# Sliding-window attention and a squared-ReLU MLP on one core: the second group's up-projection placed ahead of the first group's down-projection, which becomes seven half-size products

## The chip, the cores and the metric

One core of a Trainium2 chip runs the whole program. The metric is the device time of one execution in microseconds (us), shown as the median of three runs. Everything below on durations comes from one profiled execution of the kernel before.

## What is computed

```python
# q, k, v: [8 batches, 8 heads, 576 positions, 64] fp32
scores = (1/8) * q @ k^T
scores = where(0 <= i - j < 128, scores - slope[head] * |i - j|, -1e9)
attn   = softmax(scores) @ v
x      = attn, heads side by side: [4608 tokens, 512]
g      = maximum(x @ w_in, 0) ** 2      # w_in: [512, 2048]
out    = g @ w_out                      # w_out: [2048, 512], out fp32
```

## The kernel before

**Blocks and groups.** A batch's 576 positions are four blocks of 128 and one of 64. The kernel numbers the 40 blocks (`seq`, L351 to L364): blocks 0 to 3 are the first blocks of batches 0 to 3, and see only themselves; a later block also sees the block before it. The MLP works on nine groups of 512 tokens. Group 0 is blocks 0 to 3, group 1 is blocks 4 to 7, group 2 begins with blocks 8 and 9.

**The work on one block.** Names as in the written-out order, `m` is the block's number. `lkq` and `lv` load k, q and v from DRAM on the POOL queue and cast them to bf16 (L590, L597). For blocks 0 to 7 TensorE transposes k and q (`tp`, L653) and ScalarE or VectorE copy them out (`ev`); from block 8 on a DMA transpose on SP's queue does that (`kqT`, L638). TensorE forms the scores (`s`, L711 or L773), ScalarE the exponentials (`e`, L734), VectorE multiplies by the mask (`m`, L742), TensorE multiplies by v (`pv`, L816), VectorE takes reciprocals and divides (`r`, `n`, L832 and L845). The result is transposed into `xT`, on TensorE with a copy (`xp` at L865, then `x`) up to block 7 and by a DMA on SP (`x`, L852) after that.

**The work on one group.** Groups 0 to 2 do the up-projection as plain products (`u`, L965, grouped by `UNITS`): `u0` works on 128 tokens at a time, `u1` and `u2` on 256. Groups 3 to 8 use seven half-size products (`f`, L1059). After each come a ReLU on ScalarE (`relu`) and a square (`sq`) on either engine. The down-projection of group 0 is plain (`o`, L1137): for each of four token blocks, four parts of four matmuls 512 columns wide, then a copy (`oe`) and a store. Groups 1 to 8 use seven half-size products (`p`, L1221), each in two halves of eight matmuls 256 columns wide, with eight sums of activations on VectorE (`S1` to `S4`, L1367), copies of partial results (`s1`, `s2`, `s3`, `s5`, L443) and combining additions (`c11`, `c12`, `c22`, L1291 to L1307). These products read `wsum`, eight sums of `w_out` made once on VectorE (`ws`, L1179).

**What sets the order.** `ORDER` (L56) lists every piece of work in sequence, with its engine (none: TensorE, `a` ScalarE, `d` VectorE, `g` POOL, `s` SP) and the PSUM banks or buffers that it takes. `Plan.order` (L269) walks through that list; each engine does its own entries strictly in this order. The costs in `plan.add` (for example the 190 ns added to scores at L717) go into times that decide only how many dummy matmuls `fill` (L420) puts in front of TensorE work during the first 30 us. There are eight PSUM banks; a bank's next user waits for the last reader of the one before. k and q go through a ring of four buffers, so a load waits until the transposes of the block four loads earlier are done.

**The first 60 us of the order before.** TensorE: scores of blocks 0 to 3, `u0`, and between them the parts of `o0`, the transposes and scores of blocks 4 to 7, then `u1`, with `s8` and the first `p1` in it. POOL: `w_in` in five pieces, with `w_out0` before and `w_out1`, `w_out2` after the last of them, `w_out3` after block 5's k and q.

Of the kernel before, what the change touches and what calls it, by code (L numbers as in the profile page):

```python
# [66 lines left out]
squ0.2.2:d squ0.1.0:d u0.3.1::3 w_out3:g o0.2.0::1 tp4.0::5 tp4.1::7 squ0.1.1:d one1.7:d ev4.1.0:d squ0.0.2:d
reluu0.3.0:a:1 mask1.5:a mask0.5:a mask1.6:a mask0.6:a reluu0.0.0:a:3 ev4.0.0:a one1.3:d squ0.0.0:d u0.1.2::4
reluu0.1.2:a:0 reluu0.3.1:a:2 us3.0:d one1.0:d u0.0.3::6 reluu0.0.3:a:3 one1.8:d u0.3.2::0 s4::2,7,5,4 mask0.2:a
mask1.3:a mask0.4:a mask0.0:a mask1.0:a e4.0:a e4.3:a squ0.1.2:d squ0.0.3:d mask0.1:a mask1.7:a mask1.1:a  # L70
mask0.7:a reluu0.3.2:a:0 squ0.3.0:d squ0.3.2:d u0.2.3::3 reluu0.2.3:a:3 mask1.4:a one1.6:d squ0.2.3:d e4.1:a
u0.1.3::6 reluu0.1.3:a:1 squ0.1.3:d lkq6:g u0.0.4::2 e4.2:a o0.2.1 u0.3.3::4 o0.1.0::0 o0.1.1 o0.1.2 ws0.0:d
one1.2:d m4.3:d one1.5:d reluu0.0.4:a:0 us1.0:d m4.1:d m4.2:d tp5.0::3 tp5.1::7 lkq7:g lv5:g lv7:g lv6:g lkq8:g
lkq9:g lv8:g m4.0:d pv4.0::6 r4.0:d pv4.1::5 n4.0:d r4.1:d n4.1:d ev5.0.0:a o0.2.2 ev5.1.0:a reluu0.3.3:a:3
s5::2,3,7,6 e5.0:a e5.3:a e5.1:a e5.2:a xp4.0::4 o0.1.3 o0.2.3 tp6.0::5 tp6.1::2 lkq10:g ev6.0.0:a oe0.1.0:a:0
oe0.2.0:a:1 o0.3.0::6 tp7.0::3 tp7.1::7 st0.1.0:s lkq11:g ws0.1:d ws1.0:d x4.0:d us3.1:d us2.0:d squ0.3.3:d
m5.0:d m5.1:d ev6.1.0:d s6::4,5,2,0 e6.0:a e6.1:a e6.2:a e6.3:a ev7.1.0:a kqT8:s lv9:g kqT9:s squ0.0.4:d
ev7.0.0:d m5.3:d m5.2:d zerov10:d zerokqT10:d us0.0:d lv10:g zerov11:d o0.0.0::1 pv5.1::3 pv5.0::4 m6.0:d m6.1:d
o0.0.1 o0.0.2 kqT10:s zerokqT11:d r5.1:d r5.0:d n5.0:d n5.1:d m6.2:d squ0.3.1:d m6.3:d ws1.2:d s7::5,2,0,7
e7.0:a pv6.0::4 xp5.0::3 x5.0:a o0.0.3 pv6.1::5 e7.2:a e7.3:a e7.1:a oe0.0.0:a:2 m7.3:d m7.1:d r6.0:d m7.0:d  # L80
r6.1:d m7.2:d kqT11:s u1.0.0::3 u1.0.2::0 u1.0.3::7 pv7.0::2 pv7.1::1 r7.0:d r7.1:d n6.0:d n7.0:d n7.1:d
# [5 lines left out]
reluu1.0.6:a:1 e9.2:a m9.0:d m9.1:d m9.3:d ws0.2:d m9.2:d p1.1.0::0 u1.0.4::6 u1.0.5::5 reluu1.0.4:a:0
reluu1.1.4:a:2 s10::2,7,1,4 pv9.1::6 pv9.0::3 p1.1.1 r9.0:d r9.1:d n9.0:d e10.0:a n9.1:d squ1.0.4:d
reluu1.0.5:a:3 e10.3:a m10.3:d squ1.0.5:d us3.3:d m10.0:d s1_1:d:4 u1.1.5::2 u1.1.0::5 lkq15:g lv14:g lv11:g
lkq16:g x9:s e10.2:a e10.1:a reluu1.1.5:a:0 squ1.1.5:a s12::3,4,6,1 e12.0:a squ1.1.4:a e12.3:a st0.2.0:s kqT13:s  # L90
kqT14:s kqT16:s kqT15:s squ1.0.6:d m10.2:d u1.1.6::7 p1.2.0::2 u1.1.7::3 m12.0:d m10.1:d e12.2:a m12.2:d m12.3:d
# [5 lines left out]
lkq17:g lkq20:g x12:s x10:s x11:s u2.0.4::3 p1.5.0::5 reluu2.0.4:a:1 p1.5.1 s14::4,2,7,6 s5_1:a:5 e14.0:a
e14.1:a e14.2:a m13.2:d m13.0:d m13.1:d S4.1.0:d p1.6.0 pv13.0::3 u2.0.3::4 squ2.0.6:d squ2.0.4:d us1.1:d
m14.1:d r13.0:d m14.2:d n13.0:d m14.0:d reluu2.0.3:a:3 e14.3:a reluu2.0.1:a:1 squ2.0.0:a squ2.0.7:d p1.6.1
pv13.1::2 p1.3.0 r13.1:d n13.1:d m14.3:d s2_1:a:6 s15::7,3,4,6 pv14.0::1 pv14.1::2 r14.0:d r14.1:d us0.1:d  # L100
n14.0:d n14.1:d squ2.0.3:d lv15:g lkq18:g lkq19:g lv17:g lv18:g p1.7.0 p1.7.1 e15.0:a e15.3:a e15.2:a e15.1:a
s16::7,6,1,4 m15.0:d e16.0:a u2.1.2::2 e16.1:a e16.2:a reluu2.1.2:a:0 e16.3:a kqT17:s kqT20:s st1.2.1:s x14:s
x13:s kqT19:s u2.1.0::3 m15.1:d pv15.0::7 u2.1.3::6 reluu2.1.3:a:2 reluu2.1.0:a:3 c22_1:d us0.3:d m16.0:d
m15.2:d m15.3:d pv15.1::1 m16.1:d pv16.0::2 r16.0:d n16.0:d squ2.0.1:d r15.0:d r15.1:d p1.4.0 u2.0.2::4
u2.1.1::6 n15.0:d m16.3:d n15.1:d s17::3,2,7,1 reluu2.0.2:a:1 squ2.1.0:a m16.2:d pv16.1::4 squ2.0.2:d r16.1:d
p1.4.1 e17.0:a n16.1:d e17.3:a e17.2:a reluu2.1.1:a:1 m17.2:d squ2.1.1:d m17.3:d kqT18:s st1.2.0:s x15:s
st0.3.0:s x16:s lv19:g lkq22:g lkq21:g lkq23:g lv21:g lv20:g lkq26:g u2.1.5::3 u2.1.4::4 p1.3.1 reluu2.1.5:a:3
e17.1:a squ2.1.2:a squ2.1.5:d m17.0:d us1.3:d m17.1:d reluu2.1.4:a:1 squ2.1.3:a squ2.1.4:d c12_1:d S1.2.0:d
u2.1.7::1 u2.1.6::7 pv17.0::6 p2.1.0::3 us1.2:d S3.2.0:d r17.0:d reluu2.1.7:a:3 squ2.1.7:a reluu2.1.6:a:0
squ2.1.6:a s3_1:a:7 us0.2:d S1.2.1:d n17.0:d S2.2.1:d pv17.1::2 s18::4,5,1,7 e18.0:a e18.3:a m18.0:d ut3.0:d  # L110
p2.1.1 e18.1:a p2.2.0::0 p2.2.1 m18.1:d S2.2.0:d ut3.1:d m18.3:d ut3.2:d e18.2:a s1_2:a:0 f3.0.5::6 f3.0.1::4
p2.6.0 s5.3.0:a:1 S4.2.1:d us3.2:d r17.1:d m18.2:d s1.3.0:a:4 p2.6.1 ut3.3:d S3.2.1:d f3.0.6 f3.0.2::7
c11.3.0:d:1 p2.5.0::5 pv18.1::1 pv19.0::7 f3.0.3 s2.3.0:a:3 c11_2:d us2.2:d n17.1:d f3.0.7 pv18.0::0 s2_2:a:4
p2.7.0 p2.5.1 c12.3.0:d:2 reluc12.3.0:d c22.3.0:d:3 reluc11.3.0:a sqc11.3.0:a p2.7.1 r18.0:d r19.0:d sqc12.3.0:a
reluc22.3.0:a f3.1.1::2 s5_2:a:3 sqc22.3.0:a s1.3.1:a:1 n18.0:d S4.2.0:d r18.1:d n18.1:d n19.0:d st0.0.0:s
kqT21:s st1.3.0:s kqT22:s pv19.1::6 c22_2:d r19.1:d n19.1:d f3.0.4 kqT23:s x17:s st1.3.1:s x18:s x19:s f3.1.2::0
# [1313 lines left out]
```

## Time and profile before

| | us |
|---|---|
| median of 3 runs | 295.35 (294.89 to 295.40) |
| the profiled execution | 293.89 |
| its span, first to last instruction | 292.1 |
| TensorE busy in the span | 282.8 |
| VectorE busy | 247.1 |
| ScalarE busy | 226.9 |
| POOL busy | 106.5 |

The profiled execution lies 1.46 us below the median of the timed runs, and 1.8 us of it lie outside the span. Busy times are sums of the records of an engine. Records of matmuls overlap, since a matmul starts before the one ahead has drained: how fast a stream of them runs is read from the distance between starts, or from a merged piece of the chain (its length over its matmuls), not from the mean record.

### The profile page before, as it was taken

The page shows a single profiled execution, that of the slowest core. Times are in us where ns is not written, and L with a number is a line of the kernel's source. Part 1 is how long each engine was busy: PE and PEld are TensorE (multiplying, and loading weights), DVE is VectorE, ACT ScalarE, POOL GpSimd, SP SyncE. Part 2 cuts the span into 40 slices and gives each one's busy share as a digit, 9 for nine tenths or more (in the row PEclk, how much of TensorE's full clock was granted, in tenths as well). Part 3 has the DMA queues.
Part 4 walks back from the last instruction along what each step waited for, and adds up shares of the span by engine and source line. Part 5 has one row for each costly group of instructions (what it writes and reads, how often), then busy time and mean ns, then how long its engine had stood idle before and what let it go on. Part 6 is the DMA issues. An engine that isn't in the chain of part 4 may idle for free.

```text
span 292.1 us, 8683 instructions
## 1 busy us (share of the span) xinstructions
PE 282.8 (97%) x3443; PEld 238.5 (82%) x3443; DVE 247.1 (85%) x645; ACT 226.9 (78%) x445; POOL 106.5 (36%) x132
## 2 busy tenths in 40 slices
PE   5889999999999999999999999999999999999994
PEld 2589766788888888888888888888898888888884
DVE  4444588877798699999999999999999898999883
ACT  3658967688789695899999999899886957858710
POOL 8954377393265372912573630820000000000000
PEclk9999999999999999999999999999999999999999
DMA  9999999999999999999999999998500523010225
GB/s 124 166 199 195 190 167 179 145 130 141 180 167 143 179 207 171 131 139 173 185 173 141 142 197 154 168 168 139 116 3 5 152 80 91 1 41 20 90 81 154
DMA packets 170921, 39.64 MB, mean 136 GB/s; under 512 B 156928, under 2 KB 170368, under 8 KB 170880
## 3 DMA queue, kind: packets, MB, share of 16 engines
q0 software_dynamic: 115184, 18.10, 95.1%
q1 hardware_dynamic: 54800, 20.26, 37.6%
q10 hardware_dynamic: 896, 0.72, 1.0%
q8 instruction: 27, 0.44, 0.6%
q14 instruction: 14, 0.11, 0.1%
HBM read 36.70 MB, written 9.44 MB: 158 GB/s over the span
## 4 chain that ended last, share of the span: by engine, by line
PE 87%; DMA 8%; POOL 4%; issue 0%; ACT 0%; DVE 0%; POOLq 0%
PE o L1221 33%; PE h L1059 26%; PE h L965 13%; PE pv L816 6%; PE s L711 5%; DMA vf<-in_v_dram 3%; DMA kqT<-kq 3%; PE o L1137 2%; DMA kq<-in_q_dram 2%; POOL kq L590 2%; POOL vf L597 1%; POOL w_in_sb L535 1%; PE o L1323 1%; PE xp L865 0%; PE tp L653 0%
## 5 line engine op out<-in xcount | busy, mean ns | idle before, releaser
L734 ACT ACTIVATE P<-s 128x512 bf16<-128x512 f32 x120 | 65.6, 612 | 5.2 <-PE s L711 4.9
L1221 PEld LDWEIGHTS <-g 128*128 128x128 bf16 x624 | 60.0, 98 | 7.0
L590 POOL DMA_DIRECT2D kq<-in_k_dram x39 | 33.9, 868 | 69.4 <-DMA kqT<-kq 65.6
L932 ACT ACTIVATE rt<-h 128x512 bf16<-128x512 f32 (+1 forms) x73 | 42.3, 600 | 14.7 <-PE h L965 9.9
L1080 DVE TENSOR_TENSOR rt<-h,f 128x512 bf16<-128x512 f32 x72 | 48.7, 686 | 4.1 <-PE h L1059 1.3
L924 ACT ACTIVATE g<-rt 128x512 bf16<-128x512 bf16 x80 | 48.9, 636 | 1.4 <-DVE rt L1085 0.7
L1221 PE MATMUL o<-w_out_sb,g 128*128 128x256 bf16 x384 | 47.7, 273 | 0.0
L965 PE MATMUL h<-xT,w_in_sb 128*128 128x128 bf16 (+1 forms) x512 | 46.4, 246 | 0.0
L443 ACT ACTIVATE f<-h 128x512 f32<-128x512 f32 x59 | 34.9, 606 | 11.1 <-PE h L1059 10.9
L965 PEld LDWEIGHTS <-w_in_sb 128*128 128x128 bf16 x512 | 38.9, 98 | 3.9
L1059 PE MATMUL h<-xT,w_in_sb 128*128 128x256 bf16 x288 | 41.4, 273 | 0.1
L1059 PEld LDWEIGHTS <-w_in_sb 128*128 128x128 bf16 x384 | 35.8, 98 | 5.2 <-issue 0.3
L742 DVE TENSOR_TENSOR P<-P,masks 128x512 bf16<-128x512 bf16 x96 | 37.1, 420 | 2.2 <-ACT P L734 2.1
L597 POOL DMA_DIRECT2D vt<-in_v_dram x36 | 30.8, 876 | 16.6 <-PE pv L816 9.0
L590 POOL DMA_DIRECT2D kq<-in_q_dram x39 | 33.7, 865 | 5.7 <-DMA w_out_sb<-in_moe_w_out_dram 2.3
L926 DVE TENSOR_TENSOR g<-rt 128x512 bf16<-128x512 bf16 (+1 forms) x65 | 26.1, 415 | 6.9 <-ACT rt L932 6.6
L845 DVE TENSOR_TENSOR x<-pv,rec 128x256 bf16<-128x256 f32 (+1 forms) x80 | 31.4, 414 | 0.5
L1221 PE MATMUL o<-wsum,sums 128*128 128x256 bf16 x256 | 31.7, 273 | 0.0
L1221 PE MATMUL o<-wsum,g 128*128 128x256 bf16 x240 | 30.5, 273 | 0.0
L1059 PEld LDWEIGHTS <-us 128*128 128x128 bf16 x288 | 27.1, 98 | 3.7
L1087 ACT ACTIVATE rt<-rt 128x512 bf16<-128x512 bf16 x38 | 24.1, 637 | 5.6 <-DVE rt L1080 5.2
L816 PEld LDWEIGHTS <-P 128*128 128x128 bf16 (+1 forms) x576 | 24.0, 100 | 5.0 <-issue 2.3
(81 smaller groups left out, 398.3 us busy)
## 6 DMA issues: line engine op xcount, KB each, us to landing
out_dram<-f SPq DMA_DIRECT2D x54, 128.0 KB, 2.6
kq<-in_k_dram POOLq DMA_DIRECT2D x31, 128.0 KB, 5.9
kq<-in_q_dram POOLq DMA_DIRECT2D x31, 128.0 KB, 6.5
vt<-in_v_dram POOLq DMA_DIRECT2D x28, 128.0 KB, 7.0
w_out_sb<-in_moe_w_out_dram POOLq DMA_DIRECT2D x4, 512.0 KB, 14.5
w_in_sb<-in_moe_w_in_dram POOLq DMA_DIRECT2D x3, 512.0 KB, 10.2
out_dram<-f SPq DMA_DIRECT2D x4, 256.0 KB, 5.0
out_dram<-f SPq DMA_DIRECT2D x13, 64.0 KB, 2.1
```

Source lines behind the costliest of these rows:

```text
L443: nc.scalar.activation(o, i, AF.Copy)
L590: nc.gpsimd.dma_start(view(kq[s_kq[m].idx], i), source(src, m, split))
L597: nc.gpsimd.dma_start(tile_of(s_v[m])[0:n, :, 0:D], source(v, m))
L734: nc.scalar.activation(flat(Pt[sP.idx]), sS[i].tile.rearrange("p (j t) -> p j t", j=2)[:, :, lo:hi], AF.Exp, bias=0.0, scale=scale)
L742: nc.vector.tensor_tensor(flat(Pt[sP.idx]), flat(Pt[sP.idx]), flat(masks), op=ALU.mult)
L816: nc.tensor.matmul(sv.tile[0:n, hi * (D + 1):(hi + 1) * (D + 1)], prob, tile_of(s_v[mk])[:, h, 0:D + 1], start=mk == parts[0][1], stop=mk ...
L924: nc.scalar.activation(o, i, AF.Square, bias=0.0, scale=1.0)
L932: nc.scalar.activation(rts[srt.idx][:, 0:n], slot.tile[:, 0:n], AF.Relu, bias=0.0, scale=1.0)
L965: nc.tensor.matmul(slot.tile[:, f * w:(f + 1) * w], w_in_sb[:, cc, fc * 128:(fc + 1) * 128], xT[:, cc, lo % (XR * 128):lo % (XR * 128) + w ...
L1059: nc.tensor.matmul(slot.tile[:, j * 256:j * 256 + 256], a, b_, start=fresh and j == 0 and c == 0, stop=c == 1, skip_group_check=True)
L1080: nc.vector.tensor_tensor(rts[srt.idx], slot.tile, other(), op=ALU.add)
L1221: nc.tensor.matmul(slot.tile[:, z * 256:z * 256 + 256], stationary(c), moving(c), start=fresh and z == 0 and c == 0, stop=c == F - 1, skip ...
```

## The change

1. `G_STR` goes from 1 to 0, so that group 0's down-projection is done as the seven half-size products too. The 16 `o0` parts, four `oe0` copies and four full-width stores go; 14 `p0` halves, eight sums `S1` to `S4`, four copies, three combining additions and eight half-width stores come.
2. `ORDER` is written anew from end to end. In the first part all of `u0` and nearly all of `u1` stand ahead of `p0`; the transposes and scores of blocks 4 to 7 stand between the units of `u0`; `p1` follows `p0`.
3. On POOL the `w_out` pieces move behind the loads of blocks 4 to 7 and 9.
4. In the later groups some copies, ReLUs and squares change between ScalarE and VectorE (over the whole list 50 entries go from VectorE to ScalarE and 46 the other way). Block 0's cast of k goes to ScalarE.
5. Small edits: one 'stage' buffer for block 0's k and q becomes four entries over the same tensor `wsum` (block 0 uses the first, in the same place as before); the 190 ns in the cost of scores go; an option `SPLIT` is added and is off.

The core of the diff, with the part of the order up to the first products, as far as the prediction speaks of it:

```diff
-G_STR = 1
+G_STR = 0
...
-e1.1:a ev0.0.0:a cq0:d tp0.1::5 lv2:g pv2.0::6 r2.0:d ev0.1.0:d lv1:g lkq3:g lv0:g w_in0:g w_in1:g w_in2:g lv3:g
-w_in3:g w_out0:g lkq4:g w_in4:g w_out1:g w_out2:g lkq5:g lv4:g pv1.0::7 pv1.1::0 pv2.1::2 r1.1:d r1.0:d n1.0:d
...
+slope0.3:d cq0:d lkq1:g lv0:g lv1:g lv2:g lkq3:g w_in0:g tp2.0::1 tp0.0::2 tp0.1::3 tp2.1::4 tp1.0::5 tp1.1::6
+w_in1:g w_in2:g lv3:g w_in3:g lkq4:g lkq5:g w_in4:g lkq6:g slope1.2:a slope0.1:a slope0.0:a slope1.3:a
...
+n0.0:d b3::5,6 tp3.0::1 tp3.1::3 r2.0:d n2.0:d r0.1:d one0.1:d pv1.0::4 n0.1:d r2.1:d n2.1:d ev3.0.0:d lv4:g
+lv5:g lkq7:g lv6:g xp0.0::7 pv1.1::2 xp2.0::0 r1.1:d r1.0:d x2.0:d ev3.1.0:a s3 e3.0:a u0.2.0::3 n1.0:d n1.1:d
+x0.0:d xp1.0::1 mask1.1:a e3.1:a mask1.5:a x1.0:a u0.0.1::0 u0.0.0::4 u0.1.0::5 mask1.0:a reluu0.0.1:a:0
+reluu0.2.0:a:1 mask1.4:a reluu0.1.0:a:2 pv3.1::2 u0.0.2::7 pv3.0::6 u0.2.1::1 u0.1.1::0 dist0:d r3.0:d r3.1:d
+n3.0:d n3.1:d one1.5:d squ0.1.0:d xp3.0::3 u0.1.2::5 tp4.0::6 tp4.1::2 reluu0.2.1:a:3 squ0.2.0:d squ0.2.1:d
...
+mask0.2:a mask1.7:a reluu0.1.2:a:2 mask1.6:a ev4.0.0:d ev4.1.0:d squ0.0.1:d one1.2:d u0.2.2::1 s4::7,3,0,4
+mask0.1:a reluu0.2.2:a:0 mask0.7:a mask1.2:a e4.0:a e4.2:a mask0.6:a e4.1:a lkq9:g lv7:g w_out2:g tp5.0::6
+tp5.1::5 u0.0.3::2 u0.3.0::1 squ0.1.1:d ev5.1.0:d one1.8:d one1.7:d squ0.0.0:d one1.3:d ev5.0.0:d squ0.2.2:d
+us3.0:d one1.0:d mask0.4:a us3.1:d m4.0:d one1.1:d s5::7,5,0,6 reluu0.0.3:a:1 e4.3:a one1.4:d m4.2:d m4.3:d
+m4.1:d squ0.0.3:d e5.0:a reluu0.3.0:a:3 e5.2:a e5.1:a u0.1.3::3 u0.3.1::2 reluu0.3.1:a:0 e5.3:a tp6.0::4
+tp6.1::7 ev6.0.0:d ev6.1.0:d squ0.3.0:d u0.3.2::1 pv4.0::0 reluu0.3.2:a:1 s6::5,2,4,7 pv4.1::6 u0.2.3::1 e6.0:a
+e6.2:a e6.1:a m5.1:d m5.3:d r4.0:d m5.0:d n4.0:d r4.1:d m5.2:d n4.1:d pv5.0::5 tp7.0::0 reluu0.2.3:a:3 ev7.0.0:a
+e6.3:a pv5.1::4 m6.0:d m6.1:d r5.0:d squ0.2.3:d u0.0.4::6 xp4.0::2 tp7.1::1 reluu0.0.4:a:3 pv6.0::0 x4.0:a
+ev7.1.0:a u0.3.3::7 r5.1:d n5.0:d m6.2:d n5.1:d r6.0:d m6.3:d n6.0:d xp5.0::5 pv6.1::6 s7::4,2,0,1 x5.0:a
+lkq10:g w_out0:g w_out1:g lkq8:g squ0.3.1:d r6.1:d reluu0.3.3:a:0 n6.1:d squ0.0.4:d e7.0:a e7.3:a e7.1:a e7.2:a
+m7.0:d squ0.1.2:d squ0.3.3:d m7.1:d u1.0.3::5 u1.0.0::6 u1.0.2::7 kqT9:s m7.3:d m7.2:d us1.0:d zerokqT10:d
+kqT10:s xp6.0::4 x6.0:d u1.0.6::1 pv7.0::2 squ0.3.2:d us2.0:d r7.0:d n7.0:d pv7.1::0 u1.0.5::4 reluu1.0.3:a:3
+reluu1.0.0:a:2 squ1.0.0:a reluu1.0.6:a:0 reluu1.0.5:a:2 r7.1:d n7.1:d u1.0.4::5 xp7.0::6 u1.0.1::1 u1.0.7::2
+ws0.2:d ws0.0:d x7.0:d squ1.0.5:d w_out3:g kqT8:s lv9:g lv8:g lkq11:g lkq12:g lkq13:g lkq14:g lv12:g lv13:g
+reluu1.0.7:a:1 squ1.0.3:a squ1.0.6:a u1.1.1::0 u1.1.6::4 reluu1.1.1:a:2 reluu1.1.6:a:3 squ1.1.6:a reluu0.1.3:a:0
+S1.0.0:d u1.1.5::6 squ1.0.7:d reluu1.1.5:a:1 u1.1.3::2 u1.1.2::0 S1.0.1:d us0.0:d S3.0.1:d zerov10:d zerokqT11:d
+squ1.1.5:a u1.1.0::4 p0.1.0::3 u1.1.7::6 reluu1.1.3:a:3 us2.1:d ws0.1:d squ0.1.3:d S2.0.0:d squ1.1.3:d S3.0.0:d
...
+reluu1.0.2:a:0 squ1.0.1:d ws1.1:d reluu1.1.7:a:1 squ1.1.7:a p0.2.0::2 p0.2.1 s8::5,1,4,0 c11_0:d u1.1.4::7
+p0.5.0::6 p0.5.1 kqT11:s squ1.0.2:d S2.0.1:d S4.0.0:d e8.0:a e8.1:a e8.3:a e8.2:a m8.1:d m8.0:d s9::2,5,1,0
...
-            t = plan.add({"PE": 190.0 + len(grps) * 2 * len(pieces) * mm(128 if n == 128 else 64)}, due - 32, scores,
+            t = plan.add({"PE": len(grps) * 2 * len(pieces) * mm(128 if n == 128 else 64)}, due - 32, scores,
```

More of the change, by code (lines that the diff above doesn't have):

```diff
@@ L18 @@
 N_HW = 1
+SPLIT = False
 N_PE = 8
@@ L67 @@
[L67 to L81, printed above, removed]
@@ L87 @@
[L87 to L91, printed above, removed]
@@ L97 @@
[L97 to L116, printed above, removed]
@@ new lines @@
+S4.1.1:d r10.1:d r10.0:d n11.1:d n10.0:d n10.1:d p1.6.0 s13::1,0,2,4 e13.0:a e13.1:a e13.2:a e13.3:a kqT15:s
+st0.3.1:s x11:s x10:s st0.2.1:s x12:s u2.0.7::6 p1.5.0::5 p1.5.1 s14::1,0,2,4 reluu2.0.6:a:1 reluu2.0.7:a:3
+e14.0:a e14.2:a s5_1:a:5 p1.6.1 e14.3:a e14.1:a m13.3:d m13.0:d m13.1:d m13.2:d S4.1.0:d pv13.0::3 s2_1:d:6
+r13.0:d u2.0.0::6 u2.0.1::1 pv13.1::2 m14.2:d reluu2.0.0:a:0 squ2.0.0:a m14.1:d m14.0:d u2.0.4::4 reluu2.0.1:a:0
+lv17:g lv15:g lkq20:g lkq18:g lkq19:g n13.0:d squ2.0.7:d r13.1:d n13.1:d S3.1.1:d squ2.0.6:a p1.3.0 pv14.0::0
@@ new lines @@
+r14.0:d s15::6,3,1,2 m14.3:d n14.0:d us0.1:d p1.7.0 p1.7.1 reluu2.0.4:a:3 e15.0:a e15.3:a e15.2:a e15.1:a
+kqT17:s st0.3.0:s st0.2.0:s st0.4.2:s st0.7.3:s x13:s kqT18:s kqT20:s kqT19:s s16::4,0,6,2 u2.0.2::1 u2.1.2::3
+e16.0:a e16.2:a e16.1:a e16.3:a m15.0:d c22_1:d m15.3:d m15.2:d pv15.1::4 u2.1.3::6 pv14.1::0 m16.1:d m15.1:d
+squ2.0.4:d m16.0:d reluu2.0.2:a:1 reluu2.1.3:a:3 squ2.0.3:a reluu2.1.2:a:2 squ2.1.2:a pv15.0::2 p1.4.0 pv16.0::1
+u2.1.1::6 m16.3:d r15.0:d r14.1:d n15.0:d n14.1:d r15.1:d n15.1:d us0.3:d r16.0:d squ2.0.2:d m16.2:d n16.0:d
@@ new lines @@
+s17::2,0,3,4 p1.4.1 lkq21:g squ2.0.1:d reluu2.1.1:a:2 u2.1.4::6 pv16.1::1 e17.0:a m17.0:d us1.1:d us1.3:d
+r16.1:d n16.1:d e17.2:a x14:s x15:s st1.2.1:s x16:s st1.2.0:s st0.7.2:s squ2.1.1:d e17.3:a u2.1.0::2
+reluu2.1.4:a:1 squ2.1.4:a reluu2.1.0:a:0 e17.1:a squ2.1.3:a lv19:g lv18:g lkq23:g lkq22:g m17.1:d m17.2:d
+us3.3:d squ2.1.0:d u2.1.5::3 u2.1.6::4 reluu2.1.5:a:1 squ2.1.5:d S1.2.0:d u2.1.7::6 p1.3.1 reluu2.1.6:a:2
+reluu2.1.7:a:3 s3_1:a:7 squ2.1.7:a squ2.1.6:a lv21:g lv20:g lkq26:g s18::1,2,0,3 pv17.0::4 e18.0:a e18.2:a
@@ new lines @@
+r18.1:d pv18.0::4 r18.0:d ut3.3:d f3.1.2::5 f3.1.1::2 sqc11.3.0:a reluc12.3.0:a s2_2:a:1 p2.7.0 pv19.1::0
+sqc12.3.0:a s1.3.1:a:3 reluc22.3.0:a f3.0.4 f3.1.6 p2.7.1 S4.2.0:d c11.3.1:d:2 r19.1:d n18.0:d n18.1:d
+sqc22.3.0:a reluf3.0.4:a:0 lkq24:g lkq25:g s20::5,4,3,7 st1.3.0:s x18:s x17:s s2.3.1:a:3 reluc11.3.1:a n19.1:d
+x19:s c22_2:d sqc11.3.1:d f3.1.5::0 s5.3.1:d:4 f3.1.7 p2.3.0 e20.0:a e20.3:a e20.1:a e20.2:a m20.0:d f3.1.3
+m20.3:d c22.3.1:d:1 m20.2:d p2.4.0 m20.1:d reluc22.3.1:a sqf3.0.4:a sqc22.3.1:a c12.3.1:d:3 pv21.1::5 pv20.1::7
@@ new lines @@
+f6.0.3 S1.5.1:d ut6.2:d S2.5.1:d f6.0.7 e36.0:a e36.2:a e36.3:a e36.1:a p5.6.0 p5.6.1 s37::5,3,7,4 S4.5.0:d
+c11_5:d ut6.3:d c22.6.0:d:0 reluc22.6.0:d c12.6.0:d:1 e37.0:a e37.3:a f6.0.4 f6.2.1::0 f6.1.2::1 f6.1.1::5
+e37.1:a s1.6.1:a:0 e37.2:a reluf6.0.4:a:2 p5.5.0::4 x32:s st4.4.3:s st4.2.1:s st4.4.2:s st3.2.1:s st3.2.0:s
+x34:s st4.3.0:s st5.2.1:s x33:s x31:s x35:s st4.3.1:s st4.7.2:s p5.5.1 f6.1.6 S3.5.1:d sqc22.6.0:d c11.6.1:d:0
+m36.0:d sqf6.0.4:d m37.3:d m37.2:d S4.5.1:d m36.3:d s2_5:a:5 s2.6.1:a:0 s38::3,7,1,6 e38.0:a e38.3:a p5.7.0
@@ L214 @@
+s2_8:d:4 st7.7.3:s st7.4.3:s c12_7:d st7.3.0:s st7.3.1:s p8.7.0 p8.7.1 st7.2.1:s st8.2.1:a st8.2.0:s s5_8:a:7
+c22_8:d st8.7.3:a st8.7.2:a s3_8:d:6 p8.3.0 p8.3.1 c12_8:d st8.3.1:s st8.3.0:a p8.4.0::7 c21.0.0_8:d st8.4.0:s
+p8.4.1::2 c21.1.0_8:d st8.4.1:s p8.4.1b::6 c21.1.128_8:d st8.4.1b:a
 """
@@ L407 @@
     xt = ring("x", size["x"], [128, d_model])
-    stages = [wsum.rearrange("p s c t -> p (s c t)")[:, 0:4 * d_model].bitcast(FP32)]
-    plan = Plan({"b": 8, "f": NF, "rt": RT, **{f"g{f}.{t}": 2 for f in range(FCB) for t in range(2)}, "rec": 4, "ut": UT, "s1": 1, "s2": 1, **{f"v0.{i}": 1 for i in range(L)}, "kqT0": L, "stage": 2, **size})
+    stages = [x.rearrange("p c t -> p (c t)").bitcast(FP32) for x in (wsum[:, i] for i in range(4))]
+    plan = Plan({"b": 8, "f": NF, "rt": RT, **{f"g{f}.{t}": 2 for f in range(FCB) for t in range(2)}, "rec": 4, "ut": UT, "s1": 1, "s2": 1, **{f"stage{i}": 1 for i in range(4)}, **{f"v0.{i}": 1 for i in range(L)}, "kqT0": L, **size})
     def bank(slot, name):
@@ L566, in load_block, with fetch @@
         if split:
-            s_st = Slot("stage")
             t_l = []
+            s_st = Slot(f"stage{m % 4}")
             for i, src in enumerate((k, q)):
-                for r, (eng, e) in enumerate((("SP", nc.sync), ("SP", nc.sync) if m else ("ACT", nc.scalar))):
-                    def fetch(i=i, src=src, r=r, e=e):
-                        e.dma_start(view(stages[s_st.idx], i)[:, r], source(src, m, split)[:, :, r])
-                    t_l.append(plan.add({eng: 740.0}, key + 0.1 * i, fetch, [], [] if t_l else [s_st], dma=330.0,
-                                        lat=(1100.0 if m else 1500.0) + 600.0 * (r if m else i * (1 - r)),
+                for r in range(2):
+                    def fetch(i=i, src=src, r=r):
+                        e = nc.scalar if t_l[2 * i + r].eng == "ACT" else nc.sync
+                        e.dma_start(view(stages[m % 4], i)[:, r], source(src, m, split)[:, :, r])
+                    t_l.append(plan.add({("SP", "ACT")[r]: 720.0} if m == 0 else {"SP": 720.0, "ACT": 720.0},
+                                        key + 0.1 * i, fetch, [], [] if t_l else [s_st], dma=330.0, lat=1500.0,
                                         name=f"l{'kq'[i]}{m}.{r}", after=t_l[0] if t_l else None))
@@ L580, in cast_kq @@
                      kq[s_kq[m].idx][:, w].rearrange("s (i r d) -> s r i d", i=4, d=D),
-                     stages[s_st.idx][:, w].rearrange("s (r i d) -> s r i d", r=2, d=D))
-            engs = {"DVE": 350.0, "ACT": 480.0} if m else {"DVE": 350.0}
+                     stages[m % 4][:, w].rearrange("s (r i d) -> s r i d", r=2, d=D))
+            engs = {"DVE": 350.0, "ACT": 480.0}
             c_q = None
@@ L652, in tp @@
                 for j in range(C):
-                    nc.tensor.transpose(st.tile[:, j * 128:(j + 1) * 128],
-                                        src[:, j * 128:(j + 1) * 128], ident)
+                    nc.tensor.transpose(st.tile[:, j * 128:(j + 1) * 128], src[:, j * 128:(j + 1) * 128], ident)
             t_tp[i] = plan.add({"PE": 4 * mm(128)}, due - 60 + i, tp,
@@ L697, in job @@
         t_s = [None, None]
-        bursts = [[0, 1]]
+        bursts = [[0], [1]] if SPLIT else [[0, 1]]
         for z, grps in enumerate(bursts):
@@ L774, in scores @@
                                      tile_of(s_kqT[m])[rows, C + c, :], start=False, stop=c == C - 1)
-        t_s = plan.add({"PE": 190.0 + 4 * mm(128)}, due - 32, scores, [t_b] + t_kqT[m], name=f"s{m}")
+        t_s = plan.add({"PE": 4 * mm(128)}, due - 32, scores, [t_b] + t_kqT[m], name=f"s{m}")
         t_bias.append(t_b)
```

220 lines of the change are left out of this document (104 added, 116 removed).

## The prediction

> **What bounds the kernel now.** I read the page's busy times and slices first, then the chain that ended last (its sum, then its pieces in order of time), then TensorE's waits and timeline, then the busy times by stretch.
>
> ```profile
> PE 282.8 (97%) x3443; PEld 238.5 (82%) x3443; DVE 247.1 (85%) x645; ACT 226.9 (78%) x445; POOL 106.5 (36%) x132
> ...
> PE   5889999999999999999999999999999999999994
> ...
> PEclk9999999999999999999999999999999999999999
> ...
> PE 87%; DMA 8%; POOL 4%; issue 0%; ACT 0%; DVE 0%; POOLq 0%
> ```
>
> From the third slice (15 us) to the last TensorE is busy all the time at full clock, and 87% of the chain is TensorE. Overlapping records could hide gaps, so I look at the pieces:
>
> ```profile
> 11.50 8.59 DMA vf<-in_v_dram
> ...
> 20.53 1.79 PE h L965 x32
> ...
> 30.11 0.55 PE s L711 x16
> ...
> 34.31 0.89 PE h L965 x16
> 35.20 2.59 PE o L1137 x12
> 37.79 0.45 PE tp L653 x8
> ...
> 41.52 6.22 DMA kq<-in_q_dram
> ...
> 47.76 7.36 DMA kqT<-kq
> ...
> 275.29 11.36 PE o L1221 x104
> ```
>
> Each piece of matmuls divided by its count is the streaming rate: 56 ns at 128 columns (1.79/32), 109 at 256 (11.36/104), 216 at 512 (2.59/12). The other pieces run at these rates, so TensorE has no room. It waits in two places after its start:
>
> ```profile
> 20.13 0.40 PE L816 MATMUL pv<-vf,P 128*128 128x65 bf16 x8 [0.52 <-DMA vf<-in_v_dram]
> ...
> 55.16 0.23 PE L711 MATMUL s<-kqT,kqT 64*128 64x128 bf16 x2 [0.17 <-DMA kqT<-kq]
> ```
>
> At 20.13 block 3's v has just landed (11.50 + 8.59 = 20.09), and at 55.16 block 8's transposed k and q (47.76 + 7.36 = 55.12). Between and behind them lies one stream of work. So a change is worth what it takes from TensorE's stream after 20 us, less every wait that it adds there.
>
> **What goes and comes on TensorE.** `o0` is 64 matmuls of 512 columns: 64 x 216 = 13.8 us. `p0` is 14 x 8 = 112 of 256 columns: 112 x 109 = 12.2 us. On the path: -1.6 us. Changes between scores, `pv` and other matmuls cost about 0.1 us each (scores begin 0.1 us after the piece ahead of them ends); their number in the two orders differs by four, so I count nothing.
>
> The mean weight load is 98 ns, and one precedes every matmul. It fits below the 109 ns of a 256-column matmul, and the 104 matmuls above show it hidden. The Trainium skill ("TensorE: Matmul & The Clock Gate", section "Back-to-back issue gap") gives 81 ns per matmul for sustained streams with weight loads at 128 columns and 131 ns at 512. By a straight line between these, an estimate, `p0` would take 112 x 98 = 10.9 us and `o0` 64 x 131 = 8.4, so the change would lose 2.6 us. The rows above (56, 109, 216) disagree at every width.
>
> **What comes on the other engines.** ScalarE: four copies for four copies, nothing. VectorE: eight sums and three combining additions, records of 0.69 us, in a row 0.6 us apart: 11 x 0.6 = 6.6 us. They lie beside TensorE as long as VectorE keeps ahead of it.
>
> ```profile
> 50.00:55.00 5.00, 4.99 (x56) 4.08 (x54) 3.77 (x14) 3.61 (x7) 0.65 (x1) 1.00 1.82 153
> ...
> 60.00:65.00 5.00, 5.00 (x64) 4.42 (x62) 3.64 (x13) 4.42 (x9) 5.00 (x7) 1.00 2.11 136
> ...
> 160.00:200.00 40.00, 40.00 (x524) 34.31 (x523) 39.44 (x107) 37.52 (x73) 15.88 (x19) 1.00 1.80 162
> ```
>
> The columns are TensorE, weight loads, VectorE, ScalarE, POOL. Around 50 to 65 us VectorE is busy three quarters of the time by records that overlap a little; by its groups it idles some 22 us between 20 and 120 us, which covers 6.6. From 120 to 200 us it is nearly full and gains no work. If that cover is gone, the price is what VectorE lacks, up to 6.6 us. SP gets four more stores, behind `kqT15` and among the `x` transposes; an issue takes about 0.6 us, and blocks 10 to 16 queue behind them, far ahead of their scores. Nothing counted; one late transpose would cost under 1 us.
>
> **The start.** The new order there (k of block 0 cast on ScalarE, v ahead of block 3) ends at the same point: the same loads stand ahead of block 3's v on POOL, so it lands at 20.1 again, and TensorE has the same work done by then with the 0.52 us wait as cover. Nothing; if the start slips by more than 0.5 us, the excess is paid.
>
> **The moved loads.** Landings in the trace come 0.85 us apart for one of a block's k, q or v, half that for a 64-row block, and 2.55 us for a 512 KB weight piece, without a gap from 5 to 50 us. In the new sequence from 20.1: `w_in3` 22.6, block 4's q 24.3, block 5's 26.0, `w_in4` 28.6, block 6's q 30.3, v4 and v5 32.0, block 7's q 33.7, v6 34.5, block 9 36.2, v7 37.1, `w_out2` 39.6, block 10 40.5, `w_out0` 43.1, `w_out1` 45.6, block 8's q 47.3, `w_out3` 49.9.
>
> Against that, TensorE's list from 20.13 at rates of the chain (unit of `u0` 0.89, pair of `tp` 0.45, scores 0.55 + 0.1, half a `pv` 0.2 to 0.3, `xp` 0.22, unit of `u1` 0.87):
> - up to `tp4.1`, which needs block 4's q: four units, two `pv`, `xp`, one `tp` = 4.4, so 24.5 against 24.3;
> - to `tp5.1`: 2.0 more, 26.5 against 26.0;
> - to `tp6.1`: 4.65 more, 31.15 against 30.3;
> - to `tp7.1`: 5.2 more, 36.35 against 33.7;
> - to `p0.1.0`, which needs `w_out0` and `w_out1`: 15.85 more, 52.2 against 45.6;
> - to `p0.2.0` with `w_out3`: 2.6 more, 54.8 against 49.9;
> - to `s8`: 1.75 more, 56.6 against block 8's transposes, 47.3 + 7.36 = 54.7.
>
> Every load is there first, the first two by 0.2 and 0.5 us. ScalarE's list between 18.3 and 38 us (14 ReLUs and 16 exponentials and copies at 0.48, 13 masks at 0.2, two short ReLUs) is 17.7 us in 19.7: it runs up to 3 us behind TensorE, and by the bank numbers each bank still comes free 0.2 us or more before its next user. I take +0.2 us for these narrow places, with bounds of 0 and 1.5. The 0.17 us wait of `s8` goes; block 8 comes next late, 1.9 us away.
>
> **Sum.** -1.6 - 0.17 + 0.2 = about -1.5 us: the profiled execution's 293.89 becomes 292.4, and the median of the runs, which lies 1.46 higher, 295.35 - 1.5 = **293.9**. About 0.2%, or 0.6 us, is what a measurement can tell from no change.
>
> **Rivals.**
> - *Narrow places eat the gain.* Each of the four transposes waits on a load that must keep its pace, and ScalarE's lag holds banks. Waits of 0.9 to 2.1 us in all give 294.8 to 295.9. For it: margins of 0.2 and 0.5 us. Against: loads keep their spacing to a few hundredths, and a wait at `tp4.1` widens the margins behind it.
> - *Slower: block 8's transposes become the wait.* Its load now stands behind three `w_out` pieces, and `kqT9` and `kqT10` go ahead on SP while loads are in flight. If these two take 1.3 us each of the DMA engines (the issue record of a transpose), block 8 lands at 49.9; with the longest time to landing in the trace, 9.4 us, `s8` starts at 59.3 in place of 56.6: +2.7, and 296.6. Scores of later blocks queue behind the same transposes and could double it. It decides from a landing at 58.8 on (2.2 us late). Against: 7.36 us with eight loads in flight is the nearest row. The Trainium skill ("DMA: Bandwidth & Descriptors", section "Queues, rings and completion order") says that each DMA engine goes round its queues by packets, which fits 7.36 us beside loads.
> - *Slower: VectorE's 6.6 us are not covered.* If half meets TensorE's needs before 120 us, +3.3: 297.2. For it: it is full from 120 on. Against: 22 us of idle time ahead of that.
> - *TensorE's work does not shrink* because weight loads are not hidden between `p0` halves: 48 more loads x 98 ns = 4.7 us, so 295.35 + 4.7 - 1.5 = 298.5. The skill's rule of the sustained gap points this way; all `p` rows speak against it.
>
> **How the numbers follow.** Forecast 0.60, its own range 292.9 to 294.7; eaten gain 0.14; block 8 0.12; VectorE 0.12; no shrinking 0.02. So faster 0.60, same 0.14, slower 0.26. The range runs from 292.9 to 297.0: left out are a little of the forecast (0.03), the doubled wait (0.03), half of VectorE's case (0.06) and the last (0.02).
>
> **What will show it.** Right: L1137 gone, 112 more matmuls on L1221 at 109 ns, no TensorE wait over 0.2 us between 20 and 60 us, block 3's v at 20.1. Wrong: `tp` waiting for k or q loads, `s` at L711 waiting for `kqT`, or matmuls after 60 us waiting for VectorE; a start of the stream later than 20.6 would break the step on the start.

## The result, and the profile after

| | before | changed |
|---|---|---|
| median of 22 runs each, us | 295.14 (293.66 to 296.01) | 295.88 (294.05 to 298.15) |
| the profiled execution, us | 293.89 | 295.96 |
| its span, us | 292.1 | 294.2 |

The ratio of the times is 1.0036, with a 95% interval of 1.0018 to 1.0053: slower, by 0.7 us between the medians and 0.36% by the ratio. The prediction, 293.9, had the direction wrong; its range, 292.9 to 297.0, holds 295.88 only by what it gave to the rivals. Between the two profiled executions the gap is 2.1 us; that of before is one of its shorter ones. In the experiments a few executions ran clearly longer than the others (two of e4's six, two of e14's twelve): the medians take in all executions, the ratios and intervals leave these out.

The page of the changed kernel, from its busy times, its 40 slices and its chain:

```profile
PE 284.0 (97%) x3514; PEld 246.3 (84%) x3514; DVE 250.6 (85%) x651; ACT 228.7 (78%) x449; POOL 106.4 (36%) x132
...
PE   4899999989999999999999999999999999999995
...
PEclk9799999999999999999999999999999999999999
...
PE 83%; DMA 9%; DVE 5%; issue 1%; ACT 0%; ACTq 0%; DVEq 0%; SPq 0%
```

There are 71 more TensorE records than in the profile of before: 48 by the products (112 in place of 64) and 23 more dummy matmuls of `fill` (50 in place of 27); the 7 in the second slice of the clock and the ninth slice of PE (59 to 66 us) are new. The timeline of TensorE names every wait of 0.2 us or more that is behind the warm-up, and shows where block 3's `pv` begins:

```profile
6.35 0.40 PE L655 MATMUL tp<-ident,kq 128*128 128x128 bf16 x4 [0.62 <-DMA kq<-in_k_dram]
8.66 1.46 PE L655 MATMUL tp<-ident,kq 128*128 128x128 bf16 x12 [1.91 <-ACT kq L444]
...
21.97 0.23 PE L817 MATMUL pv<-vf,P 128*128 128x65 bf16 x2
...
59.90 0.23 PE L712 MATMUL s<-kqT,kqT 64*128 64x128 bf16 x2 [1.43 <-DMA kqT<-kq]
```

Two waits are new. At 8.66 TensorE has waited 1.91 us for block 0's k, whose second half is now the second load on ScalarE's queue (landing 6.60; in the kernel before the first, 3.76) and whose cast on ScalarE has the 1.28 us loading of its table between. Block 3's v has landed at 19.90, but TensorE gets to it at 21.97 in place of 20.13. And at 59.90 block 8's scores have waited 1.43 us for their transposes. Of the chain, in order of time, the pieces that lead there and some of `p0` behind:

```profile
37.16 13.73 DMA kq<-in_q_dram
...
50.96 8.89 DMA kqT<-kq
59.85 0.05 issue
59.90 0.62 PE s L712 x16
```

```profile
61.50 1.75 PE o L1222 x16
64.39 3.49 PE o L1222 x32
```

Block 8's q was issued at 37.16 and landed at 50.90; its transposes landed at 59.85. From there TensorE hardly waits to the end: 294.2 - 59.9 = 234.3 us, where the prediction had 290.6 - 56.6 = 234.0. So the whole miss lies ahead of `s8`, which starts 3.3 us later than forecast. The pieces of `p0` run at 109 ns (3.49 over 32), as its step said.

**Theory** for the experiments: block 8's transposes set the start of `s8`, because the DMA transposes of blocks 9 and 10, in flight on SP's queue from 36.7 and 41.0 us, slow the loads that block 8 needs. **Rivals**: the late start is what costs the time; the loads' order does; VectorE's added work does; the products save nothing.

### The profile page after: what moved, and what is told of

It reads as the page before. It is cut to its first block, busy times and chain, and to the rows that moved or that the text cites. A ratio compares the mean times of both kernels' runs of the same rounds, so it can differ in the third digit from the quotient of the medians.

```text
span 294.2 us, 8852 instructions
## 1 busy us (share of the span) xinstructions
PE 284.0 (97%) x3514; PEld 246.3 (84%) x3514; DVE 250.6 (85%) x651; ACT 228.7 (78%) x449; POOL 106.4 (36%) x132
## 3 DMA queue, kind: packets, MB, share of 16 engines
q1 hardware_dynamic: 55248, 20.13, 39.3%
## 4 chain that ended last, share of the span: by engine, by line
PE 83%; DMA 9%; DVE 5%; issue 1%; ACT 0%; ACTq 0%; DVEq 0%; SPq 0%
PE o L1222 35%; PE h L1060 23%; PE h L966 9%; PE pv L817 6%; PE s L712 5%; DMA kq<-in_q_dram 5%; DMA kqT<-kq 3%; DMA wsum<-in_k_dram 2%; DVE rt L1081 1%; PE tp L655 1%; PE tp L423 1%; PE s L765 1%; PE o L1324 1%; DVE P L743 1%; PE s L774 0%
## 5 line engine op out<-in xcount | busy, mean ns | idle before, releaser
L1222 PEld LDWEIGHTS <-g 128*128 128x128 bf16 x704 | 67.5, 98 | 8.2
L735 ACT ACTIVATE P<-s 128x512 bf16<-128x512 f32 x120 | 64.0, 616 | 5.4 <-PE s L712 5.4
L925 ACT ACTIVATE g<-rt 128x512 bf16<-128x512 bf16 x88 | 53.2, 631 | 1.3 <-DVE rt L1086 0.5
L1222 PE MATMUL o<-w_out_sb,g 128*128 128x256 bf16 x432 | 54.1, 273 | 0.0
L1222 PE MATMUL o<-wsum,sums 128*128 128x256 bf16 x288 | 36.2, 273 | 0.0
L1222 PE MATMUL o<-wsum,g 128*128 128x256 bf16 x272 | 34.8, 273 | 0.0
L1222 PEld LDWEIGHTS <-sums 128*128 128x128 bf16 x288 | 27.7, 98 | 3.3
L444 ACT ACTIVATE f<-o 128x512 f32<-128x512 f32 x30 | 17.9, 597 | 13.4 <-PE o L1222 13.4
L1088 ACT ACTIVATE rt<-rt 128x512 bf16<-128x512 bf16 x40 | 25.2, 635 | 3.0 <-DVE rt L1081 2.9
```

Source lines behind the costliest of these rows:

```text
L444: nc.scalar.activation(o, i, AF.Copy)
L735: nc.scalar.activation(flat(Pt[sP.idx]), sS[i].tile.rearrange("p (j t) -> p j t", j=2)[:, :, lo:hi], AF.Exp, bias=0.0, scale=scale)
L925: nc.scalar.activation(o, i, AF.Square, bias=0.0, scale=1.0)
L1222: nc.tensor.matmul(slot.tile[:, z * 256:z * 256 + 256], stationary(c), moving(c), start=fresh and z == 0 and c == 0, stop=c == F - 1, skip ...
```

## The experiments

Each stands beside runs of the kernel before on its own chip; the ratio is to those. There are 12 executions of each, but 6, 5 and 4 of e4, e5 and e6.

| kernel | median us | ratio, 95% interval |
|---|---|---|
| e1_start_back | 296.68 | 1.0050 (1.0028 to 1.0072) |
| e4_block8_load | 299.25 | 1.0102 (1.0054 to 1.0149) |
| e5_both | 300.94 | 1.0211 (1.0184 to 1.0239) |
| e6_both_no_dummies | 301.26 | 1.0218 (1.0188 to 1.0247) |
| e7_transposes_behind | 294.17 | 0.9989 (0.9967 to 1.0011) |
| e8_behind_and_start | 294.17 | 0.9992 (0.9965 to 1.0020) |
| e9_plain_o0 | 296.31 | 1.0046 (1.0023 to 1.0069) |
| e10_no_late_dummies | 294.64 | 1.0008 (0.9985 to 1.0032) |
| e11_changed_again | 295.97 | 1.0035 (1.0017 to 1.0053) |
| e12_block10_behind | 295.68 | 1.0044 (1.0014 to 1.0074) |
| e13_block10_and_start | 295.59 | 1.0031 (1.0004 to 1.0059) |
| e14_behind_again | 294.59 | 0.9989 (0.9959 to 1.0018) |
| e15_load8_between | 295.42 | 1.0011 (0.9983 to 1.0038) |
| e16_load8_between_start | 295.11 | 1.0011 (0.9985 to 1.0038) |

### The start taken back

```diff
-... lk0.0:s lq0.1:a one0.0:d warm0:d warm::0 lkq2:g lk0.1:a lq0.0:s ck0:a
+... lk0.0:s lk0.1:a one0.0:d warm0:d warm::0 lkq2:g lq0.0:s lq0.1:a ck0:d
```

> The changed kernel with two edits of its start taken back: block 0's k halves are both loaded ahead of its q halves, and its cast goes back to VectorE. Start theory (the stream is late at block 3's v, 21.97 instead of 20.13 us, only because TensorE waits 1.91 us for that cast and then runs at a granted clock of 0.50 from 9 to 12 us): no wait for the cast, clock 1.00 from 5 us on, block 3's `pv` begins by 20.6, and, if nothing behind it holds the gain back, 1.8 us less: 294.1. Together with the block 8 theory (block 8's scores start when its transposes land, 59.85 us, and these depend on the DMA queues and not on TensorE): the 1.4 us wait of `s8` grows to about 3.2, `s8` still starts at 59.9, and the time stays within 0.4 us of the changed kernel's. Rival (the time is lost to VectorE's added sums or behind 60 us): block 3's `pv` is earlier, the wait of `s8` does not grow, and the gain vanishes at waits for VectorE.

The timeline of TensorE in this kernel (e1), and then its busy times around 60 us (TensorE, weight loads, VectorE, ScalarE, POOL, granted clock, DMA share, GB/s):

```profile
20.06 0.28 PE L817 MATMUL pv<-vf,P 128*128 128x65 bf16 x4 [0.52 <-DMA vf<-in_v_dram]
59.24 0.23 PE L712 MATMUL s<-kqT,kqT 64*128 64x128 bf16 x2 [2.70 <-DMA kqT<-kq]
```

```profile
58.00:60.00 2.00, 0.76 (x17) 0.56 (x18) 0.88 (x2) 0.32 (x1) 0.27 (x1) 0.89 2.20 153
60.00:62.00 2.00, 2.00 (x12) 1.45 (x11) 0.99 (x3) 1.77 (x5) 2.00 (x3) 0.50 1.36 121
```

The start is whole again: block 3's `pv` at 20.06 (21.97 as changed) with the 0.52 us wait of the kernel before. The wait of `s8` grows from 1.43 to 2.70, and `s8` begins only 0.66 us earlier. So the late start is not what the time was lost to: block 8's transposes are a floor that TensorE reaches sooner or later. I had not expected that even the 0.66 us would be lost. The second fence shows it: after the longer wait the granted clock is 0.50, and from `s8` to the next block's scores it takes 4.90 us (59.24 to 64.14) in place of the changed kernel's 3.28 (59.90 to 63.18), 1.6 more. This execution is 1.1 us longer than the changed kernel's (spans of 295.3 and 294.2). Over all executions a rise is not shown: the ratios to the kernel before are 1.0050 and 1.0036, with intervals that overlap.

### Block 8's load earlier, alone and with the start, and without dummies

```diff
-lkq10:g w_out0:g w_out1:g lkq8:g
+lkq10:g lkq8:g w_out0:g w_out1:g
```

> The changed kernel with the load of block 8's q and k put ahead of the first two pieces of w_out instead of behind them. Block 8 theory: the load lands some 7 to 8 us earlier (about 43 in place of 50.9), its transposes by 53, the 1.43 us wait of `s8` goes, the span falls by 1.4 us and the time to about 294.5. Price to watch: w_out's second piece lands up to 2 us later (48.35 to 50.2), while the first `p0` that needs it begins at 53.9, so nothing. Rival (the transposes of block 8 are slow because of the loads beside them, wherever its load stands): `s8` still waits over 1 us and the time does not move.

> Both edits together: the start taken back and block 8's load ahead of w_out. If the start (1.84 us) and block 8's wait (1.43 us) are all that the prediction missed, apart from dummy matmuls (about 0.4 us), the time falls by 3.3 us to about 292.6, 2.5 below the kernel before, and the profile shows no TensorE wait over 0.2 us from 20 to 62 us. Rival (VectorE's eight sums and three combinations, 6.6 us, are not covered): TensorE waits for VectorE appear, and the time stays at 294.5 or more.

The last one (e6) has `FILL = 0.0` as well:

> As the last one, with all dummy matmuls left out (52 of them, 7 behind 20 us). The seven behind 20 us stand in the stream and cost 7 x 56 ns = 0.4 us. Those ahead of it either fill waits (then taking them out gives nothing, and the waits become idle time) or delay the stream. Theory: 0.4 us less, about 292.2. Rival: with more idle time in the first 20 us the granted clock falls to 0.50 there as it did in the changed kernel, and the time rises by 0.5 to 1.7 us.

All three missed. Timelines, first TensorE's and VectorE's with block 8's load moved (e4), then the same two with both edits (e5):

```profile
50.06 5.40 PE L966 MATMUL h<-xT,w_in_sb 128*128 128x256 bf16 x48 [1.47 <-DVE xT L442]
```

```profile
48.38 1.29 DVE L1180 TENSOR_TENSOR wsum<-w_out_sb 128x1024 bf16<-128x1024 bf16 x2 [2.35 <-DMA w_out_sb<-in_moe_w_out_dram]
```

```profile
53.46 7.28 PE L966 MATMUL h<-xT,w_in_sb 128*128 128x256 bf16 x48 [6.46 <-DVE xT L442]
```

```profile
51.78 1.29 DVE L1180 TENSOR_TENSOR wsum<-w_out_sb 128x1024 bf16<-128x1024 bf16 x2 [7.34 <-DMA w_out_sb<-in_moe_w_out_dram]
```

The wait of `s8` is gone in both, and a worse one stands in its place. I had looked for the first user of `w_out` on TensorE (`p0` at 53.9). The first on VectorE is `ws0.2`, at 46, and the copy `x7` that TensorE needs for `u1` stands behind it in VectorE's list. w_out's first piece lands at 48.36 in the one and 51.75 in the other (44.25 as changed). The times of e4 spread from 296.19 to 302.37, and its profile is of the shortest, so how long this wait mostly is isn't seen. In e5, w_out's first piece is spread over eight microseconds: the first of its 16 parts lands at 43.43, the last at 51.75, with block 9's transpose in flight beside it (36.28 to 50.32). e6 waits 6.64 us at the same place; its granted clock stays at full speed in the first 20 us, so the drop that its rival had there did not come, but what the dummies are worth can't be read from a kernel with such a wait. What follows: the order of the loads can't be mended by moving block 8's alone, since w_out's first piece has no slack either.

### The transposes of blocks 9 and 10 behind block 8's

```diff
-... u1.0.2::7 kqT9:s m7.3:d m7.2:d us1.0:d zerokqT10:d
-kqT10:s xp6.0::4 ...
+... u1.0.2::7 m7.3:d m7.2:d us1.0:d
+xp6.0::4 ...
-w_out3:g kqT8:s lv9:g
+w_out3:g kqT8:s kqT9:s zerokqT10:d kqT10:s lv9:g
```

> The changed kernel with SP's DMA transposes of blocks 9 and 10 put behind that of block 8; its start and its loads stay as changed. Transpose theory (a DMA transpose in flight takes turns with the loads packet by packet: beside block 9's, the two w_out pieces landed 4 us apart in place of 2.55): w_out's first two pieces land at about 43.1 and 45.6, block 8's q at 47 to 48 in place of 50.9, its transposes by 55 to 57, ahead of the 58.5 at which TensorE wants them: the 1.43 us wait goes, the span falls to 292.8 and the time to about 294.5. Rival (the loads themselves crowd the DMA engines, whatever the transposes do): block 8's q lands at 50 or later, `s8` still waits over 1 us, and blocks 9 and 10 wait as well: 296 to 299.

> The changed kernel again, unchanged, for a second profile and for times on the same chip as the next three. Transpose theory: `s8` waits over 1 us again, for block 8's transposes, and the time is 295.9 within 0.4. The wait for the cast of k at the start (1.91 us) stands in the first profile and in the one with block 8's load moved (1.65), but not in the one with the transposes behind; here it may be there or not, and the start of `s8` should not follow it.

> The kernel with the transposes of blocks 9 and 10 behind block 8's once more, beside the changed kernel on one chip: 1.5 to 1.8 us less than the changed kernel, as before (294.17 against 295.88), if that difference is the transposes' and not a chip's.

Only SP's order is changed (and the place of one short memset on VectorE), and the time falls by 1.7 us by the medians and 1.4 by the ratios (1.0036 and 0.9989, intervals apart), and by 1.4 again in the repeat on one chip (e11 and e14: 1.0035 and 0.9989, intervals that just touch). In the trace of e7 w_out's first two pieces land at 43.22 and 45.77, 2.55 apart again (44.25 and 48.35 as changed); block 8's q at 47.50 in place of 50.90 (47.3 predicted); its transposes at 53.68 in place of 59.85; `s8` begins at 56.53 (56.6 predicted) and does not wait. The second profile of the changed kernel (e11) repeats the first: block 8's q lands at 50.87, its transposes at 60.44, and `s8` waits 1.37 us. TensorE's waits in the two executions with the transposes behind, e7 with its `s8` and then e14:

```profile
20.11 0.28 PE L817 MATMUL pv<-vf,P 128*128 128x65 bf16 x4 [1.21 <-DMA vf<-in_v_dram]
...
56.53 0.23 PE L712 MATMUL s<-kqT,kqT 64*128 64x128 bf16 x2
...
69.56 0.23 PE L712 MATMUL s<-kqT,kqf 64*128 64x128 bf16 x2 [1.25 <-DVE P L750]
```

```profile
6.44 0.40 PE L655 MATMUL tp<-ident,kq 128*128 128x128 bf16 x4 [0.70 <-DMA kq<-in_k_dram]
8.28 1.17 PE L655 MATMUL tp<-ident,kq 128*128 128x128 bf16 x12 [1.45 <-ACT kq L444]
```

The same program has a late start in one execution and not in the other: block 0's second half of k landed at 4.37 in the first. Both spans end alike, 292.3 and 292.4. The execution with the good start (`s8` at 56.53 against 58.04) gives its gain back at 69.56 (69.75 in the other), at block 12's scores. The page names VectorE there, but in all six executions that wait at this place (e7, e8, e9, e10, e15, e16) they start 0.13 to 0.14 us after block 12's transposes land (69.42 here): it is the next DMA floor. Block 12's load waits for the buffer of block 9, and so is issued at 56.6 in place of 49.3.

### The start, the products and the late dummies without the first floor

> The same with the start taken back as well (block 0's k loaded first, cast on VectorE). If the transposes behind block 8's remove the floor under `s8`, the 1.84 us of the start now count: `s8` begins at about 56.7, 3.2 us earlier than in the changed kernel, and the time is about 292.7, some 2.5 below the kernel before. If the floor stays (transposes landing at 59 to 60), the time is the changed kernel's or up to 1 us more, as with the start alone.

The next (e9) has `G_STR = 1`, with `o0.0.0` to `o0.3.3` for the `p0` halves, four `oe0` for the copies, and the sums and combinations of group 0 taken out:

```diff
-p0.1.0::3 ... p0.1.1 s1_0:a:0 ... p0.2.0::2 p0.2.1 ... c11_0:d
+o0.0.0::3 ... o0.0.1 ... o0.0.2 o0.0.3 ... oe0.0.0:a:0
```

> The last one with the first group's down-projection plain again, its sixteen parts in the places of the fourteen half-size products; the eight sums and three combinations on VectorE go. If the products are worth what their rows say (64 x 216 against 112 x 109 ns) and VectorE's 6.6 us are covered: 1.6 us slower than the last one, about 294.3. If the added work on VectorE eats it: no slower than the last one, or faster.

The third (e10) has `FILL_UNTIL = 20000.0` in place of 30000.0:

> The same as the one with the transposes behind and the start taken back, without the seven dummy matmuls behind 20 us: 7 x 56 ns = 0.4 us less where nothing else is late, about 292.3; no change if TensorE then waits at `tp4` or at `s8`.

With the start taken back (e8) the median does not move; `s8` begins at 56.16, and 1.11 us of it go at block 12, whose transposes land at 68.91 (in this execution, one of its longer ones, two more waits for transposes, 1.5 us together, and one of 1.1 us for an `x` follow):

```profile
69.05 0.23 PE L712 MATMUL s<-kqT,kqf 64*128 64x128 bf16 x2 [1.11 <-DMA kqT<-kq]
```

The plain `o0` is 2.1 us slower by the medians, 1.6 by the ratios (0.0054 x 295), and their intervals do not overlap: the products are worth what their rows say, and VectorE's added work is covered. The dummies are not to be measured: 294.64 against 294.17, 0.4 expected the other way, with runs that spread over 2.5 us.

### One transpose ahead, and an earlier load for block 12

```diff
-w_out3:g kqT8:s lv9:g
+w_out3:g kqT8:s zerokqT10:d kqT10:s lv9:g
```

> The changed kernel with only the DMA transpose of block 10 put behind that of block 8; block 9's stays ahead. Transpose theory: half of the 3.4 us by which the two delayed block 8's load goes; its q lands at about 49, its transposes by 57, the wait of `s8` is under 0.3 us, and block 12's load, which waits for block 9's buffer, is earlier than with both behind (56.5), so the 1.25 us wait of block 12's scores there is smaller too: 293 to 294. Rival (block 9's transpose alone does the damage): as the changed kernel, 295.9.

> The same with the start taken back too. If nothing holds `s8` any more, its time is that of the last one or up to 1.8 us less in executions whose start is late there: 292.5 to 294. If `s8` is held by its transposes once TensorE comes earlier, no gain.

The forecast of e12 missed and its rival held: 295.68 us, against 295.9. Of e13, the branch without a gain came. Block 9's transpose alone holds block 8's q back to 49.58 (47.50 with none ahead, 50.90 with two), and block 8's transposes take 8.73 us to land, nearly as long as in the changed kernel:

```profile
49.65 8.73 DMA kqT<-kq
```

```profile
58.42 0.23 PE L712 MATMUL s<-kqT,kqT 64*128 64x128 bf16 x2 [2.01 <-DMA kqT<-kq]
```

```profile
58.55 0.23 PE L712 MATMUL s<-kqT,kqT 64*128 64x128 bf16 x2 [2.45 <-DMA kqT<-kq]
```

The first two fences (chain, then timeline) are of the kernel with block 10's behind, the third of the one with the start taken back too. `s8` starts at nearly the same time in both, though TensorE is there 0.3 us earlier in the second (56.10 against 56.41): the floor once more.

The last two (e15, e16) have both transposes behind, and block 8's load one place earlier:

```diff
-lkq10:g w_out0:g w_out1:g lkq8:g
+lkq10:g w_out0:g lkq8:g w_out1:g
```

> The kernel with the transposes of blocks 9 and 10 behind block 8's, and block 8's load moved up between w_out's first two pieces; start as changed. Theory (block 12's scores wait for transposes that land at 69 us, since block 12's load is issued only when block 9's transposes have given back their buffer, at 56.6): block 8's q lands near 45, block 9's transposes by 54, block 12's load is issued 2 to 2.5 us earlier, its transposes land at about 67, no TensorE wait over 0.3 us at block 12, span about 291.5 to 292.4, time 293.4 to 294.2. w_out's second piece lands up to 4 us later (45.6 to 49.5), still ahead of 52. Rival (TensorE ends up waiting for something else, such as w_out's second piece behind a transpose): 295 or more.

> The same with the start taken back. If block 12 was what swallowed the start: 0.5 to 1.5 us less than the last one, 292.3 to 293.4, and 1.5 to 2.5 below the kernel before. If there is no difference again, another wait holds TensorE between block 8 and the end, and the profile names it.

Block 8's q lands at 45.26 as hoped, but block 9's transposes at 57.51, not by 54: issued 2.2 us earlier than in e7 (46.73 against 48.97), they take 10.78 us in place of 7.11. Block 12's load is issued at 58.04 and its transposes land at 70.55, later than before, and in e16 at 69.03, where its scores start at 69.17. Earlier loads did not bring the transposes forward, so this way does not lift the second floor, and whether the start's 1.8 us would show without it stays open. No version was shown to beat the kernel before: with the transposes behind, the interval is 0.9967 to 1.0011.

## Why the prediction was wrong, step by step

- **TensorE's work, -1.6 us: right.** The pieces of `p0` run at 109 ns, the stretch from `s8` to the end is 234.3 us where 234.0 was forecast, and the plain `o0` costs 1.6 to 2.1 us.
- **The moved loads: this step failed**, in its line on `s8`: "56.6 against block 8's transposes, 47.3 + 7.36 = 54.7". The 2.55 us between weight pieces was read where no transpose was in flight. With two in flight the second of the two pieces came 4.1 us behind the first (3.5 in e11), block 8's q landed at 50.90 and its transposes took 8.89 us: 59.85, not 54.7. With these two out of the way the load and `s8` come within 0.2 us of the working (47.50 and 56.53), the transposes 1.0 earlier than it has them (53.68). "Without a gap from 5 to 50 us" was too smooth a reading, too: in the trace of before one weight piece landed 3.15 us behind the load ahead of it (35.08), and a v of a full block 2.07 in place of 0.85 (55.22), beside the transposes of block 8 and those behind them. The last of these was a sign that loads and transposes in flight together land late.
- **The rival named it.** "Block 8's transposes become the wait" has the place and the mechanism, and 59.3 against 59.90 for `s8`; 296.6 us against the median of 295.88. That it comes so near is in part luck: it priced the two transposes at 2.6 us from the length of their issue records, and they cost 3.4 of landing (50.90 against its 49.9), while its 9.4 us for block 8's own transposes was 0.5 more than they took. It had a chance of 0.12 because the 7.36 us was taken as "the nearest row", which is that of a transpose with no other one ahead.
- **The start, "nothing": wrong in the profiled execution, and without effect.** "The excess is paid" was wrong: TensorE was 1.84 us late, and hidden behind the floor at 59.85. The working looked at the loads and at the amount of TensorE's work, and not at what the first transposes wait for.
- **Narrow places, +0.2:** at `tp4` to `tp7` there is no wait of 0.2 us. What I had not counted are seven dummy matmuls at 26.01 and 31.06, 7 x 56 ns = 0.4 us; whether they cost time the runs can't tell.
- **VectorE's 6.6 us: covered**, as said: no wait of TensorE for VectorE over 0.2 us in the changed kernel, and taking the sums away with the products made it slower by what TensorE's rows say. **Weight loads: hidden**, as said.
- **A reading of the page:** "from the third slice" TensorE is not yet busy all the time. That slice (14.6 to 21.9 us) is an 8, with waits of 0.52 us at 15.31 and 20.13; the 9s begin with the fourth. No term of the sum rests on it.
- **Turns.** In the changed kernel 311 transpose packets went beside 302 weight packets from 42 to 44 us, by the trace's packets, about one for one. The Trainium skill ("DMA: Bandwidth & Descriptors", section "Queues, rings and completion order") has a DMA engine go round its queues by packets, and this agrees. I cited it for the calm side, though it spoke for the rival: a transpose that takes turns with loads makes them late.

## What to carry to other kernels

Where a trace shows a wait ended by a DMA, time saved ahead of it is worth nothing until that landing moves too: work out the landing first, with every transfer that the new order puts in flight beside it, transposes on other queues included. A spacing of loads read from one stretch holds only for the same mix of transfers. And before a load is moved back, look for its first user on every engine, and at what stands behind that user in the engine's list.
